# Late stores, four chunks ahead of the weights, and decay columns and more layouts by DMA in a fused decay-attention and feed-forward kernel

## The chip, the cores and the metric

One core of a Trainium2 chip. The metric is the device time of one execution in microseconds (us); a smaller one is better. The kernel before took 193.73 us (median of three runs, 192.81 to 193.88) in its first measurement. Its runs are of two kinds: those with a mean granted TensorE clock of 1.0 take 191.3 to 192.5 us, those with 0.99 mostly 192 to 194 us. So every comparison below is between runs of one session on one chip, and differences below half a percent are not read.

TensorE is PE below, VectorE DVE, ScalarE ACT, GpSimd POOL, SyncE SP. SP computes nothing here: it issues the loads of the operands, the transposes by DMA and (some of) the stores, one after the other in program order.

## The reference

Attention with a decayed state, 4 sequences, 8 heads, 768 steps, head size 48; then a feed-forward layer with squared ReLU.

```python
f = 1.0 / (1.0 + np.exp(-f_logit))
for t in range(S):
    state = f[:, :, t, :, None] * state + np.einsum('bhd,bhe->bhde', k[:, :, t], v[:, :, t])
    y[:, :, t] = np.einsum('bhd,bhde->bhe', q[:, :, t], state)
x = y.transpose(0, 2, 1, 3).reshape(B * S, H * D)      # 3072 x 384
h = np.maximum(x @ w_in, 0.0)                          # 384 -> 2048
return h * h @ w_out                                   # 2048 -> 384
```

## The kernel before

The 3072 steps are 24 chunks of 128, six to a sequence. `UNITS` says which chunks go through the first layer together, by first chunk and number. A small planner in the program takes each step of each chunk with its engine, its estimated length, its predecessors and the buffers that it takes and gives, and puts the instructions of all engines into one order. In the first 40 us it also puts "fillers" into PE's gaps: matmuls on zeros whose result nobody uses.

The order of loads. A weight slice (0.393 MB in the chip's type, four of `w_in`, four of `w_out`) is issued by POOL behind the cast of the v of the chunk named last but one before it:

```python
LOADS = [0, "i0", 1, "i1", 2, "i2", 3, "i3", 4, "o0", "o1", 5, "o2", "o3"] + list(range(6, NCH))
XBAR = 14      # from this chunk on, q and k are transposed by DMA and not by PE
XBAR2 = 18     # from this chunk on, the attention result is transposed by DMA
UNITS = [(0, 2), (2, 1), (3, 1), (4, 1), (5, 1)] + [(c, 3) for c in range(6, NCH, 3)]
# ... cut
plan.add(f"cw{kind}{s}", "POOL", 1.0, fn, after=[f"vc.{behind}"], rank=-1, data=(2.4, 0))
```

The decay. `pc` holds the running sum of log decays: 384 columns for the steps, and four one-column matmuls more that give the whole chunk's decay as a column for each pair of heads. One exponential on ACT turns all 388 columns into factors, DVE multiplies q with them, POOL multiplies the state by the last four.

```python
nc.tensor.matmul(pc[:, :HD], ut, pt[:, :, :D])
if not last:
    for pr in range(NP):
        nc.tensor.matmul(pc[:, HD + pr:HD + pr + 1], pt[:, 2 * pr:2 * pr + 2, :]..., ones)
# ... cut
nc.scalar.activation(st["en", i][:, :w], st["pc", i][:, :w], AFT.Exp, scale=-1.0)
# ... cut: the state update, on POOL
nc.gpsimd.tensor_mul(nx[r, ...], st["tm", i][r, ...], st["en", i][r, HD:HD + NP]...to_broadcast([D, NP, D]))
plan.add(f"s2.{i}", "POOL", 1.0, s2, after=[f"s1.{i}"] + ([f"p4.{i - 1}"] if c else []), ...)
```

The stores leave as each chunk is done, 18 through POOL and the last six through SP, from four output buffers:

```python
soft = i < NCH - 6
(nc.gpsimd if soft else nc.sync).dma_start(out[i * C:(i + 1) * C, :], st["ob", i])
```

## Time and profile before

| | before |
|---|---|
| median of the first session | 193.73 us (3 runs) |
| profiled run | 191.61 us, span 189.8 us, clock 1.000 |
| PE busy | 93% of the span, fillers included |
| PE work, from start-to-start times | 160.2 us |
| PE's last matmul ends, by the same count | 186.2 us |
| so PE lost | 26.0 us: 16.5 in 0 to 25 us, 6.7 in 25 to 50, 1.8 in 50 to 100, 1.0 after 100 |

The prediction below shows the lines that carry this. Two more are wanted for comparison, the rows of granted clock and of DMA bandwidth in 40 slices of the span of before (4.7 us each):

```profile
PEclk9999999999999999999999999999999999999999
GB/s 122 188 191 206 174 187 153 196 164 191 205 137 221 232 227 201 207 197 159 140 155 194 207 137 241 218 109 215 194 216 177 176 60 64 62 45 41 41 41 83
```

The clock is never throttled in this run, and the DMA engines move some 190 GB/s, 109 in the weakest slice, until slice 31.

### The profile page before, as it was taken

The page shows a single profiled execution, that of the slowest core. Times are in us where ns is not written, and L with a number is a line of the kernel's source. Part 1 is how long each engine was busy: PE and PEld are TensorE (multiplying, and loading weights), DVE is VectorE, ACT ScalarE, POOL GpSimd, SP SyncE. Part 2 cuts the span into 40 slices and gives each one's busy share as a digit, 9 for nine tenths or more (in the row PEclk, how much of TensorE's full clock was granted, in tenths as well). Part 3 has the DMA queues.
Part 4 walks back from the last instruction along what each step waited for, and adds up shares of the span by engine and source line. Part 5 has one row for each costly group of instructions (what it writes and reads, how often), then busy time and mean ns, then how long its engine had stood idle before and what let it go on. Part 6 is the DMA issues. An engine that isn't in the chain of part 4 may idle for free.

```text
span 189.8 us, 4807 instructions
## 1 busy us (share of the span) xinstructions
PE 177.5 (93%) x1845; PEld 120.8 (64%) x1845; DVE 127.6 (67%) x259; ACT 132.8 (70%) x281; POOL 54.8 (29%) x105
## 2 busy tenths in 40 slices
PE   6978689989899999999999999999999999999992
PEld 5867478767676666665656666666565666666551
DVE  5484688668397886999988777777667764343300
ACT  4426479786676469999998986978875787565521
POOL 5451343241224561305324311531324401100000
PEclk9999999999999999999999999999999999999999
DMA  6999899999979999999799999979999762211112
GB/s 122 188 191 206 174 187 153 196 164 191 205 137 221 232 227 201 207 197 159 140 155 194 207 137 241 218 109 215 194 216 177 176 60 64 62 45 41 41 41 83
DMA packets 118646, 30.26 MB, mean 159 GB/s; under 512 B 113408, under 2 KB 117760, under 8 KB 118624
## 3 DMA queue, kind: packets, MB, share of 16 engines
q1 hardware_dynamic: 113760, 23.27, 71.2%
q0 software_dynamic: 4864, 6.69, 16.4%
q8 instruction: 14, 0.23, 0.5%
q14 instruction: 8, 0.07, 0.1%
HBM read 25.17 MB, written 4.72 MB: 157 GB/s over the span
## 4 chain that ended last, share of the span: by engine, by line
PE 75%; ACT 11%; DMA 4%; SPq 3%; DVE 3%; issue 2%
PE op L489 31%; PE hp L444 30%; ACT hr L451 4%; DMA io_f<-in_f_logit_dram 4%; SPq L215 3%; PE at L342 3%; PE yp L365 3%; PE tr L318 2%; ACT hT L458 2%; PE pc L286 2%; PE xp L379 1%; PE ds L405 1%; ACT pz L276 1%; ACT e L275 1%; DVE hr L453 1%
## 5 line engine op out<-in xcount | busy, mean ns | idle before, releaser
L444 PE MATMUL hp<-xT,w_in 128*128 128x384 bf16 (+2 forms) x528 | 78.0, 282 | 2.5 <-DVE hr L453 1.9
L489 PE MATMUL op<-w_out,hT 128*128 128x384 bf16 x384 | 76.2, 326 | 0.3 <-ACT ob L499 0.3
L451 ACT ACTIVATE hr<-hp 128x384 bf16<-128x384 f32 (+1 forms) x100 | 50.5, 509 | 20.0 <-PE hp L444 18.0
L444 PEld LDWEIGHTS <-w_in 128*128 128x128 bf16 x528 | 42.3, 98 | 20.7 <-issue 4.0
L489 PEld LDWEIGHTS <-hT 128*128 128x128 bf16 x384 | 35.1, 98 | 21.8 <-issue 0.4
L460 DVE TENSOR_TENSOR hT<-hr 128x384 bf16<-128x384 bf16 (+1 forms) x75 | 29.7, 400 | 27.7 <-ACT hr L451 26.8
L349 DVE TENSOR_TENSOR am<-at,ut 128x512 bf16<-128x512 f32 x48 | 31.6, 685 | 3.7 <-PE at L342 3.4
L422 POOL TENSOR_TENSOR sz<-tm,en 48x192 bf16<-48x192 f32 x40 | 22.0, 549 | 29.9 <-DVE tm L413 7.2
L458 ACT ACTIVATE hT<-hr 128x384 bf16<-128x384 bf16 (+1 forms) x45 | 24.8, 554 | 1.6 <-DVE hr L453 0.3
L504 POOL DMA_DIRECT2D out_dram<-ob x18 | 10.4, 577 | 47.3 <-ACT ob L499 31.2
L280 POOL CAST vz<-io_v 128x384 bf16<-128x384 f32 x24 | 13.6, 567 | 31.2 <-DMA io_v<-in_v_dram 30.7
L306 DVE TENSOR_TENSOR az<-io_k,ep 128x384 bf16<-128x384 f32 x24 | 14.0, 584 | 8.3 <-ACT ep L296 5.1
L275 ACT ACTIVATE e<-io_f 128x384 f32<-128x384 f32 x24 | 12.5, 520 | 7.7 <-DMA io_f<-in_f_logit_dram 7.7
L499 ACT COPY ob<-op 128x384 f32<-128x384 f32 x18 | 8.6, 478 | 12.8 <-PE op L489 12.7
L296 ACT ACTIVATE ep<-pc 128x384 f32<-128x384 f32 x24 | 11.7, 486 | 5.8 <-PE pc L289 5.4
L310 DVE TENSOR_TENSOR az<-io_q,en 128x384 bf16<-128x384 f32 x24 | 14.7, 614 | 0.0
L276 ACT ACTIVATE pz<-e 128x384 bf16<-128x384 f32 x24 | 12.5, 523 | 0.8
L453 DVE TENSOR_SCALAR hr<-hp 128x384 bf16<-128x384 f32 (+1 forms) x20 | 11.6, 584 | 2.0 <-PE hp L444 1.8
L522 PE MATMUL idle<-zero 128*128 128x128 bf16 x119 | 11.9, 256 | 1.0 <-DVE zero L245 1.0
L302 ACT ACTIVATE en<-pc 128x388 f32<-128x388 f32 (+1 forms) x24 | 11.8, 491 | 0.0
L326 DVE COPY ts<-tr 128x1024 bf16<-128x1024 bf16 x14 | 9.6, 687 | 3.1 <-PE tr L318 2.7
L365 PE MATMUL yp<-vz,am 128*128 128x48 bf16 x192 | 9.5, 184 | 1.3 <-DVE am L349 0.8
(40 smaller groups left out, 149.4 us busy)
## 6 DMA issues: line engine op xcount, KB each, us to landing
io_f<-in_f_logit_dram SPq DMA_DIRECT2D x24, 192.0 KB, 4.5
io_k<-in_k_dram SPq DMA_DIRECT2D x24, 192.0 KB, 4.6
io_q<-in_q_dram SPq DMA_DIRECT2D x24, 192.0 KB, 4.5
io_v<-in_v_dram SPq DMA_DIRECT2D x24, 192.0 KB, 4.5
out_dram<-ob POOLq DMA_DIRECT2D x18, 192.0 KB, 3.5
w_in<-in_moe_w_in_dram POOLq DMA_DIRECT2D x4, 384.0 KB, 7.4
w_out<-in_moe_w_out_dram POOLq DMA_DIRECT2D x4, 384.0 KB, 6.9
out_dram<-ob SPq DMA_DIRECT2D x6, 192.0 KB, 1.9
```

The costliest lines, as they stand in the source:

```text
L275: nc.scalar.activation(e, st["f", i].rearrange("p h d -> p (h d)"), AFT.Exp, scale=-1.0)
L276: nc.scalar.activation(pz[i % 2][:, :, :D], e.rearrange("p (h d) -> p h d", d=D), AFT.Ln, bias=1.0)
L306: nc.vector.tensor_mul(az[i % 4][:, H:, :D], st["k", i], st["ep", i])
L310: nc.vector.tensor_mul(az[i % 4][:, :H, :D], st["q", i], st["en", i][:, :HD].rearrange("p (h d) -> p h d", d=D))
L349: nc.vector.tensor_mul(t, st["at", i][x], ut4)
L365: nc.tensor.matmul(o_, w, r, start=(n == 0), stop=(n == len(ops) - 1), skip_group_check=True)
L422: nc.gpsimd.tensor_mul(nx[r, :, D * x:D * (x + 1)], st["tm", i][r, :, D * x:D * (x + 1)], st["en", i][r, HD:HD + NP].unsqueeze(2).to_broad ...
L444: nc.tensor.matmul(hp[:, x, :], w_in[:, ks, (f + x) * C:(f + x + 1) * C], xT[:, ks, lo:lo + W], start=(ks == 0), stop=(ks == KS - 1), skip ...
L451: nc.scalar.activation(hr[:, :m, :], st["hp", c0, f][:, :m, :], AFT.Relu)
L458: nc.scalar.activation(st["hT", g][:, f:f + m, lo:lo + W], hr[:, :m, :], AFT.Square)
L460: nc.vector.tensor_mul(st["hT", g][:, f:f + m, lo:lo + W], hr[:, :m, :], hr[:, :m, :])
L489: nc.tensor.matmul(st["o", i], hT[:, fs, tt * C:(tt + 1) * C], w_out[:, fs, :], start=(fs == 0), stop=(fs == FS - 1))
```

## The change

Its intent: take 2.6 us of small matmuls and transposes from PE and let the DMA engines do them, pay for their time by moving the stores behind the last load, and give PE more attention work at the start by loading four chunks before any weight.

```diff
-    LOADS = [0, "i0", 1, "i1", 2, "i2", 3, "i3", 4, "o0", "o1", 5, "o2", "o3"] + list(range(6, NCH))
+    LOADS = [0, 1, 2, 3, "i0", "i1", "i2", "i3", "o0", "o1", 4, "o2", "o3"] + list(range(5, NCH))
-    XBAR = 14
-    XBAR2 = 18
-    UNITS = ... + [(c, 3) for c in range(6, NCH, 3)]
+    XBAR = 12
+    GX = 9
+    XBAR2 = 14
+    UNITS = ... + [(c, 3) for c in range(6, NCH - 3, 3)] + [(c, 1) for c in range(NCH - 3, NCH)]
 ... the column matmuls of the decay
-            if not last:
+            if not last and i < GX:
 ... the exponential, from chunk 9: written transposed, so that its last row can be sent to a column
+                t = t.rearrange("p (x d n) -> p x d n", x=2, n=NP)
+                t, st["row", i] = t[:, :, :D].rearrange("p x d n -> p n x d"), t[C - 1:C]
+                nc.scalar.activation(t, st["pc", i][:, :HD]..., AFT.Exp, scale=-1.0)
 ... the transfer
+        def tg():
+            t = st["g", i] = work.tile([C, NP], F32, tag="g", bufs=3, name="g")
+            nc.sync.dma_start(t, st["row", i].rearrange("o x d n -> o (x d) n"))
+        if i >= GX:
+            plan.add(f"tg.{i}", "SP", 0.45, tg, after=[f"a2n.{i}"], take=["g"], rank=-2, data=(0.2, 128))
 ... the stores: all on SP, behind the last load, from 20 buffers (OBB) instead of 4
-                (nc.gpsimd if soft else nc.sync).dma_start(out[i * C:(i + 1) * C, :], st["ob", i])
+                nc.sync.dma_start(out[i * C:(i + 1) * C, :], st["ob", i])
-            plan.add(f"d{i}", "POOL" if soft else "SP", ..., after=[f"e{i}"], rank=-1, ...)
+            plan.add(f"d{i}", "SP", 0.45, dma, after=[f"e{i}", f"v{LATE}"], rank=1, ...)
```

Cut: buffers for the exponential and for g, three planning lengths on PE, and a test in the planner's model of the DMA queue.

More of the change, by code (lines that the diff above doesn't have):

```diff
@@ L113, in order @@
                         us, size = s.data
-                        while sum(z for e, z in queue if e > end) + size > self.RING:
+                        while size and sum(z for e, z in queue if e > end) + size > self.RING:
                             end = min(e for e, z in queue if e > end)
@@ L175 @@
     NCH = B * NC
+    LATE = NCH - 1
+    OBB = 20
     IOB = 7
     HTB = 3
-    LOADS = [0, "i0", 1, "i1", 2, "i2", 3, "i3", 4, "o0", "o1", 5, "o2", "o3"] + list(range(6, NCH))
+    LOADS = [0, 1, 2, 3, "i0", "i1", "i2", "i3", "o0", "o1", 4, "o2", "o3"] + list(range(5, NCH))
     LOADS = [x if isinstance(x, int) else (x[0], int(x[1])) for x in LOADS]
     FILL = 40.0
-    XBAR = 14
-    XBAR2 = 18
-    UNITS = [(0, 2), (2, 1), (3, 1), (4, 1), (5, 1)] + [(c, 3) for c in range(6, NCH, 3)]
+    XBAR = 12
+    GX = 9
+    XBAR2 = 14
+    UNITS = [(0, 2), (2, 1), (3, 1), (4, 1), (5, 1)] + [(c, 3) for c in range(6, NCH - 3, 3)] + [(c, 1) for c in range(NCH - 3, NCH)]
     GC = 3
@@ L198 @@
     plan.buffers(**{"io_" + n: IOB for n in "fkqv"})
-    plan.buffers(m=2, tr=1, at0=1, at1=1, h=2, o=1, hr=3, hT=HTB, xT=2, ob=4,
-                pz=2, az=4, vz=4, ts=3, am=2, ys=3, ep=2, en=4)
+    plan.buffers(m=2, tr=1, at0=1, at1=1, h=2, o=1, hr=3, hT=HTB, xT=2, ob=OBB,
+                pz=2, az=4, vz=4, ts=3, am=2, ys=3, ep=2, en=4, g=3)
     st = {}
@@ L254 @@
         nc.gpsimd.tensor_copy(ut4[:, j, :], ut)
-    pz, az, vz, sz = [], [], [], []
+    pz, az, vz, sz, ez = [], [], [], [], []
     for j in range(2):
@@ L263 @@
         nc.vector.memset(az[j], 0.0)
+        ez.append(const.tile([C, H * DP], F32, name=f"ez{j}"))
+        nc.gpsimd.memset(ez[j], 0.0)
         vz.append(const.tile([C, H, D], BF16, name=f"vz{j}"))
@@ L291, in p1 @@
             st["pc", i] = pc
-        plan.add(f"p1.{i}", "PE", 0.26, p1, after=[f"a1.{i}"] + ([f"p4.{i - 3}"] if i > 2 else []), take=["m"], give=[f"pz:a1.{i}"], rank=rank)
+        plan.add(f"p1.{i}", "PE", 0.26 if i < GX and not last else 0.165, p1, after=[f"a1.{i}"] + ([f"p4.{i - 3}"] if i > 2 else []), take=["m"], give=[f"pz:a1.{i}"], rank=rank)
         def a2p():
@@ L299, in a2n @@
         def a2n():
-            w = HD if last else HD + NP
-            st["en", i] = work.tile([C, HD + NP], F32, tag="en", bufs=4, name="en")
-            nc.scalar.activation(st["en", i][:, :w], st["pc", i][:, :w], AFT.Exp, scale=-1.0)
+            t = ez[i % 4]
+            if i < GX:
+                w = HD if last else HD + NP
+                nc.scalar.activation(t[:, :w], st["pc", i][:, :w], AFT.Exp, scale=-1.0)
+                st["en", i], st["g", i] = t[:, :HD].rearrange("p (h d) -> p h d", d=D), t[:, HD:HD + NP]
+            else:
+                t = t.rearrange("p (x d n) -> p x d n", x=2, n=NP)
+                t, st["row", i] = t[:, :, :D].rearrange("p x d n -> p n x d"), t[C - 1:C]
+                nc.scalar.activation(t, st["pc", i][:, :HD].rearrange("p (n x d) -> p n x d", x=2, d=D), AFT.Exp, scale=-1.0)
+                st["en", i] = t
         plan.add(f"a2n.{i}", "ACT", 0.37, a2n, after=[f"p1.{i}", f"a2p.{i}"], take=["en"], give=[f"m:p1.{i}"])
@@ L309, in v1q @@
         def v1q():
-            nc.vector.tensor_mul(az[i % 4][:, :H, :D], st["q", i], st["en", i][:, :HD].rearrange("p (h d) -> p h d", d=D))
+            t, z = st["q", i], az[i % 4][:, :H, :D]
+            if i >= GX:
+                t, z = (y.rearrange("p (n x) d -> p n x d", x=2) for y in (t, z))
+            nc.vector.tensor_mul(z, t, st["en", i])
         plan.add(f"v1q.{i}", "DVE", 0.47, v1q, after=[f"a2n.{i}", f"q{i}", f"v1k.{i}"], give=[f"io_q:q{i}"] + ([f"en:a2n.{i}"] if last else []))
@@ L344, in p3 @@
             st["am", i] = [None, None]
-        plan.add(f"p3.{i}", "PE", 0.34, p3, after=[f"v2.{i}"], take=["at0", "at1"], rank=rank)
+        plan.add(f"p3.{i}", "PE", 0.42, p3, after=[f"v2.{i}"], take=["at0", "at1"], rank=rank)
         def v3(x):
@@ L366, in p4 @@
             st["yp", i] = yp
-        plan.add(f"p4.{i}", "PE", 0.38 if c else 0.2, p4, after=[f"v3b.{i}", f"vc.{i}"] + ([f"s2.{i - 1}"] if c else [])
+        plan.add(f"p4.{i}", "PE", 0.37 if c else 0.2, p4, after=[f"v3b.{i}", f"vc.{i}"] + ([f"s2.{i - 1}"] if c else [])
                  + ([] if last else [f"p5.{i}"]),
@@ L422, in s2 @@
                 nc.gpsimd.tensor_mul(nx[r, :, D * x:D * (x + 1)], st["tm", i][r, :, D * x:D * (x + 1)],
-                                     st["en", i][r, HD:HD + NP].unsqueeze(2).to_broadcast([D, NP, D]))
-        plan.add(f"s2.{i}", "POOL", 1.0, s2, after=[f"s1.{i}"] + ([f"p4.{i - 1}"] if c else []), give=[f"en:a2n.{i}"])
+                                     st["g", i][r].unsqueeze(2).to_broadcast([D, NP, D]))
+        def tg():
+            t = st["g", i] = work.tile([C, NP], F32, tag="g", bufs=3, name="g")
+            nc.sync.dma_start(t, st["row", i].rearrange("o x d n -> o (x d) n"))
+        if i >= GX:
+            plan.add(f"tg.{i}", "SP", 0.45, tg, after=[f"a2n.{i}"], take=["g"], rank=-2, data=(0.2, 128))
+        plan.add(f"s2.{i}", "POOL", 1.0, s2, after=[f"s1.{i}"] + ([f"p4.{i - 1}"] if c else []) + ([f"tg.{i}"] if i >= GX else []),
+                 give=[f"en:a2n.{i}"] + ([f"g:tg.{i}"] if i >= GX else []))
     def mm1(c0, n):
@@ L497, in ev, with dma @@
             def ev(e, i=i):
-                ob = st["ob", i] = ffp.tile([C, d_model], F32, tag="ob", bufs=4, name="ob")
+                ob = st["ob", i] = ffp.tile([C, d_model], F32, tag="ob", bufs=OBB, name="ob")
                 copy[e](ob, st["o", i])
-            soft = i < NCH - 6
-            def dma(i=i, soft=soft):
-                (nc.gpsimd if soft else nc.sync).dma_start(out[i * C:(i + 1) * C, :], st["ob", i])
+            def dma(i=i):
+                nc.sync.dma_start(out[i * C:(i + 1) * C, :], st["ob", i])
             both(f"e{i}", 0.46, 0.37, ev, after=[f"o{i}.4"], take=["ob"], give=[f"{tag}:o{i}.0"])
-            plan.add(f"d{i}", "POOL" if soft else "SP", 1.0 if soft else 0.45, dma, after=[f"e{i}"], give=[f"ob:e{i}"], rank=-1, data=(0.6, 0 if soft else 128))
+            plan.add(f"d{i}", "SP", 0.45, dma, after=[f"e{i}", f"v{LATE}"], give=[f"ob:e{i}"], rank=1, data=(0.6, 128))
     for i in range(NCH):
```

## The prediction

> **What bounds the kernel now.** I read the page's shares first, then the waits of the TensorE, then its timeline, then the DMA queues in the first 50 us. The page:
>
> ```profile
> PE 177.5 (93%) x1845; PEld 120.8 (64%) x1845; DVE 127.6 (67%) x259; ACT 132.8 (70%) x281; POOL 54.8 (29%) x105
> ...
> DMA  6999899999979999999799999979999762211112
> ```
>
> TensorE (PE) is busy 93%, but 11.9 us of that are fillers (the group idle<-zero, x119), all before 40 us. The DMA row is full until slice 31 (about 150 us) and nearly empty after it. So there are two regimes: a start in which PE has too little to do because operands and weights are still coming, and a long stretch in which PE is the bound. The waits of PE alone confirm it; these are the largest two of all:
>
> ```profile
> PE hp L444 <- DVE hr L453: 1.9, 1, 1.9
> PE pc L286 <- ACT pz L276: 1.8, 3, 1.0
> ```
>
> Both lie before 30 us. Between 50 and 187 us PE stands idle in the records for under 1 us (busy 49.64 of 50, 50.00 of 50, 36.40 of 37). A busy PE need not be at its peak, so I check by start-to-start times in the PE timeline (columns: start, length, line, operation, count):
>
> ```profile
> 50.61 0.83 PE L444 MATMUL hp<-xT,w_in 128*128 128x128 bf16 x12
> 51.28 1.14 PE L489 MATMUL op<-w_out,hT 128*128 128x384 bf16 x6
> ...
> 53.41 0.61 PE L318 MATMUL tr<-ident,az 128*128 128x128 bf16 x8
> 53.86 0.33 PE L405 MATMUL ds<-vz,az 128*128 128x96 bf16 x4
> ...
> 59.60 0.24 PE L289 MATMUL pc<-ones,pz 128*128 128x1 bf16 x4
> 59.71 0.33 PE L379 MATMUL xp<-ident,ys 128*128 128x128 bf16 x3
> ...
> 178.44 7.96 PE L489 MATMUL op<-w_out,hT 128*128 128x384 bf16 x48
> ```
>
> Twelve 128-column matmuls take 51.28 - 50.61 = 0.67 us, 56 ns each; the last 48 of 384 columns take about 163 ns each. Both scale with columns, so nothing but issue stands between them: PE streams. From 49.67 us to its last matmul at 186.4 us it has 136.8 us, of which I count 133 us as matmuls at such rates; the rest is mostly 0.1 us ahead of each chunk's L342. **What counts is therefore PE work after the start plus what PE fails to do in the start.** Loads, stores, DVE and ACT count only if they starve PE.
>
> **What the skill says.** (1) "Perfetto Trace Analysis", Identifying the Most-Contended Engine: matmul busy share is a poor measure, weight-load share a better one. Here that is 64% against 93%; 384-column matmuls need one load each, so I trust the start-to-start times. (2) "TensorE: Matmul & The Clock Gate", section "Wait — 56ns, not 53.3ns?": 128 columns cost 55.6 ns warm, columns at 2.4 GHz plus about 2.5 ns. The trace agrees: 56 ns. (3) "DMA: Bandwidth & Descriptors", Queues, rings and completion order: each DMA engine takes turns between queues at packet granularity, so a queue with large packets gets more bytes. The trace agrees in direction, in the queue view of 10 to 18 us, where the first three weight slices (software queue) run beside operand loads (hardware queue); columns are packets, MB, time share:
>
> ```profile
> q0 software_dynamic: 1117, 1.11, 83.3%
> q1 hardware_dynamic: 2330, 0.44, 36.6%
> ```
>
> Weights move 0.139 MB/us, loads 0.055 MB/us, against 0.18 to 0.19 for loads alone. (4) Same page, "Issuing engines are not separate DMA queues": moving a DMA to another issuer saves only issue time. No run shows this yet; I use it for the stores.
>
> **The change, part by part.**
>
> Decay by DMA from chunk 9. The four one-column matmuls (L289) cost 59.71 - 59.60 = 0.11 us a chunk. They go in chunks 9 to 22 except 11 and 17 (a sequence's last chunk has none): 12 x 0.105 = **-1.26 us** of PE. A tiny DMA per chunk takes their place, and the state update waits for it. Median landing of other DMAs on that queue is 4 to 5 us in this busy phase, but chunks come some 6 us apart and other matmuls fill the wait.
>
> Operand transposes by DMA from chunk 12 instead of 14: eight matmuls cost 53.86 - 53.41 = 0.45 us; two chunks, **-0.90 us**. Two DVE copies of 0.69 us go too, off the path. Result transposes from chunk 14 instead of 18: 0.17 us each (three 56 ns matmuls), four chunks, **-0.68 us**.
>
> Last three chunks one at a time: 144 matmuls of 128 columns replace 48 of 384. Per 384 columns 3 x 56 = 168 ns instead of 163, plus rounding: some **+0.24 us**. The last group may start before chunk 23 is through, but PE already had work there (no wait after 150 us), so this gains nothing.
>
> Sum: -1.26 - 0.90 - 0.68 + 0.24 = **-2.6 us of PE in the saturated stretch**.
>
> Stores after the loads. 18 stores leave POOL, where each issue took 0.58 us. They took 3.54 MB out of the loaded phase; at about 0.19 MB/us plus the lighter cost of their large packets I estimate 10 us of DMA, against some 7 us for two more operand and four more result transposes (1.7 and 0.9 us, the kernel's own plan; an estimate). Loads end a few us earlier. PE was not waiting for loads, so: **0**. In the tail 24 stores of 0.2 MB in 35 us are no load; the last store is unchanged.
>
> Four chunks ahead of the weights. POOL's timeline of before, casts of v and weight issues:
>
> ```profile
> 7.02 0.50 POOL L280 CAST vz<-io_v 128x384 bf16<-128x384 f32 x1 [3.50 <-DMA io_v<-in_v_dram]
> 7.46 1.69 POOL L231 DMA_DIRECT2D w_in<-in_moe_w_in_dram  x2
> ...
> 21.63 0.94 POOL L280 CAST vz<-io_v 128x384 bf16<-128x384 f32 x1 [6.62 <-DMA io_v<-in_v_dram]
> 22.51 0.80 POOL L231 DMA_DIRECT2D w_in<-in_moe_w_in_dram  x1
> 27.33 0.51 POOL L280 CAST vz<-io_v 128x384 bf16<-128x384 f32 x1 [0.24 <-DMA io_v<-in_v_dram]
> 27.78 1.55 POOL L233 DMA_DIRECT2D w_out<-in_moe_w_out_dram  x2
> ```
>
> Weight slices were let go by the casts of chunks 0, 0, 1, 2, 3, 3, 4, 4; now all six first ones wait for chunk 2 and the last two for chunk 3. Chunks 0 and 1 landed 4.2 us apart undisturbed, so chunk 2 now lands near 15.5 us, not 21.6. Weights then flow from about 18 us (packets came 2 us after issue), w_in complete after 4 x 0.393 / 0.139 = 11.3 us: 29.5 us (before: about 29). w_out moved 0.80 MB in 8 us per pair, so it ends near 45.5 us (before: 46). The total is the same; the order is the difference. What PE can do meanwhile: attention of 0 to 3 is through by 22 us, about 4 us earlier. But the first ReLU on ACT comes behind chunk 4's exponential in program order, and f of chunk 4, squeezed to 0.055 MB/us, lands only near 27 us. I expect PE to stall around 23 to 28 us, then to run full until it waits for the last w_out slices near 41 to 45 us. PE work done at 46 us: attention 0 to 4 (9 us), first layer of 0 to 4 (13 us), second layer of chunk 0 (2.6 us), 24.5 us; before it was about 25. **0 within 3 us.** I choose 0.3 us of gain, from fewer small waits; the choice is weak.
>
> Total: 193.7 - 2.6 - 0.3 = **190.8 us**.
>
> **Rivals.** (a) The start gains 3 to 4 us: if loads keep a larger share beside the weights, chunk 4 lands by 24 us, the ReLUs are not blocked, and PE enters saturation with more done. For it: weights in the w_out phase left loads 0.07 to 0.08 MB/us, and fewer back-and-forth waits. Then 187 to 188. (b) The start loses: six weights in a row starve chunks 3 and 4, and the blocked ACT and DVE hold the two hp buffers, as DVE did at 19.5 us (the 1.9 us wait). Then 193 to 195. (c) A new wait replaces the removed work: the decay DMA, queued in order behind loads on SP, delays the state update and so L365, or SP stands waiting for it and loads come late; chunk 23's transposes stand behind up to 16 stores. For it: f of chunk 23 was issued at 142.6 and used at 148.3 us, no great lead. Against: PE found other work through all such waits before. Up to +2 us. (d) The removed matmuls hid under others: against it stand the start-to-start times above.
>
> **Range and chances.** The PE sum is safe to 0.5 us; the start carries +-3 us, new waits up to +2. Hence 187.5 to 194.0. Faster by over 2% needs 189.86 or less, 0.9 us below my centre: 0.36. Slower by over 2% needs 197.6, three things failing at once: 0.04. Within 2%: 0.60.
>
> **What would show it.** Right: L289's count 80 to 32, tr 112 to 96, xp 54 to 42; PE still without waits from 50 us to the end; PE's last matmul about 2.5 us earlier; DMA row emptying earlier, then stores. Fillers and waits before 46 us about equal in sum, with a gap at 23 to 28 us. Wrong: PE saturated before 42 us or only after 50 us; PE waits on L365, L342 or on sz after 90 us; a gap near the end behind a chunk 22 or 23 transpose.

## More of the kernel before

"PE work" is a count: each matmul at the start-to-start time that its shape shows in the busy stretch (0.163 us for 384 columns, 0.109 for 256, 0.056 for 128, 0.0265 for one column, and so on), fillers at nothing. What is left of the time until PE's last matmul is "lost". Work plus loss is the end, so a change that takes work away gains only if the loss stays.

## The result

The changed kernel took 195.38 us (median of 4 runs, 195.06 to 195.61), the kernel before 193.41 us (4 runs, 192.81 to 193.88) on the same chip. The ratio is 1.010, with a 95% interval of 1.007 to 1.014: 1% slower, where 1.5% faster was predicted, and outside the predicted range. A later session gave 1.011 (1.005 to 1.018).

| | before | after |
|---|---|---|
| profiled span, clock | 189.8 us, 1.000 | 193.3 us, 0.982 |
| PE work | 160.2 us | 157.6 us |
| PE lost, 0 to 25 us | 16.5 | 18.4 |
| 25 to 50 us | 6.7 | 7.6 |
| 50 to 100 us | 1.8 | 4.4 |
| after 100 us | 1.0 | 1.5 |
| last load issued | 147.8 us | 154.5 us |

The work fell by 2.6 us, exactly as predicted. The loss rose by 5.8 us in the profiled runs. The profiled run of before was a quick one (191.61 us, against a median of 193.41); by the medians, 2.0 us slower with 2.6 us less work, the loss rose by some 4.6 us. From the page of the changed kernel, shares and the rows that answer to those of before:

```profile
PE 178.8 (93%) x1861; PEld 124.0 (64%) x1861; DVE 128.8 (67%) x252; ACT 132.3 (68%) x274; POOL 47.5 (25%) x91
...
PEclk9999969879999999999999999999999999999999
DMA  6999999999999944979997799979988989671012
GB/s 119 192 178 173 175 189 185 184 169 202 169 196 167 178 73 84 194 145 169 158 203 145 124 197 167 153 152 175 151 158 168 154 216 293 223 271 43 33 52 79
```

The shares say nothing: PE is 93% busy in both. The rows say where to look: a clock that falls in slices 5 to 8 (24 to 43 us), and a hole in the DMA row at slices 14 and 15 (68 to 77 us), while loads are still wanted. PE's largest waits in the changed kernel (who waited, for what, us in total, times, longest):

```profile
PE tr L333 <- DVE az L325: 2.6, 1, 2.6
PE hp L467 <- DMA w_in<-in_moe_w_in_dram: 1.9, 1, 1.9
```

The first layer waits for its first weights, at 24.3 us, where it started at 17.1 us in before (its matmuls on `w_in` up to 60 us, before and after: ns at least, in the median, at most; first and last start):

```profile
L444 PE MATMUL hp<-xT,w_in x240: 216/219/283, 17.1 to 56.0; 128*128 128x128 bf16 x96, 128*128 128x256 bf16 x24
L467 PE MATMUL hp<-xT,w_in x192: 216/219/421, 24.3 to 50.5; 128*128 128x128 bf16 x144, 128*128 128x256 bf16 x48
```

Then the transposes of chunk 4 wait for their operand, at 37.4 us. POOL's timeline of the changed kernel shows the cause of both (start, length, operation; idle time before):

```profile
16.34 0.51 POOL L285 CAST vz<-io_v 128x384 bf16<-128x384 f32 x1 [1.68 <-DMA io_v<-in_v_dram]
16.88 3.24 POOL L234 DMA_DIRECT2D w_in<-in_moe_w_in_dram  x4
20.12 1.52 POOL L236 DMA_DIRECT2D w_out<-in_moe_w_out_dram  x2
...
23.26 1.54 POOL L236 DMA_DIRECT2D w_out<-in_moe_w_out_dram  x2
...
42.20 0.51 POOL L285 CAST vz<-io_v 128x384 bf16<-128x384 f32 x1 [12.91 <-DMA io_v<-in_v_dram]
```

The chunk 2 cast comes at 16.3 us, near the predicted 15.5. Then all eight slices are asked for within 8 us, and the v of chunk 4 lands only at 42.2 us, against 36.9 us in before. The DMA queues of the changed kernel, 24 to 30 us (packets, MB, share of the time):

```profile
q0 software_dynamic: 974, 0.95, 93.2%
q1 hardware_dynamic: 969, 0.18, 27.8%
```

The two queues moved the same number of packets, 974 and 969 (and 1174 each in 30 to 36 us). That agrees with the turn by packets that the Trainium skill describes in "DMA: Bandwidth & Descriptors", Queues, rings and completion order, though a profile's packet need not be what the page calls one, and how many go in one turn is not seen. With weights always outstanding, loads get one packet of 190 bytes for every weight packet of 980 (both are means), 0.03 MB/us. The prediction took 0.055 MB/us from a window in which loads had moved two packets for each weight packet, because the weight queue was empty at times.

The wait itself is not all. In the windows of the changed kernel around the two waits (start:end, length, busy time and count by engine, then granted clock, DMA share, GB/s):

```profile
22.00:28.00 6.00, 4.07 (x49) 3.48 (x48) 2.85 (x6) 1.90 (x4) 2.66 (x5) 0.72 1.21 191
28.00:36.00 8.00, 6.38 (x85) 5.53 (x83) 3.02 (x8) 7.01 (x14) 1.04 (x2) 1.00 1.26 186
36.00:42.00 6.00, 4.58 (x42) 3.68 (x43) 3.46 (x7) 1.80 (x4) 0.00 (x0) 0.72 1.25 194
```

A mean of 0.72 over 6 us fits half a clock for 3.4 us (1 - 0.5 x 3.4 / 6 = 0.72). In before the clock is 1.00 in these three windows. Both dips follow a wait of 2 to 3 us.

The hole at 68 to 77 us. SP's largest wait but one, and SP's timeline across it, in the changed kernel:

```profile
SPq L443 <- ACT ez L313: 8.3, 5, 5.9
```

```profile
66.16 1.01 SPq L218 DMA_DIRECT2D io_k<-in_k_dram  x1
73.11 0.56 SPq L443 DMA_DIRECT2D g<-ez  x1
73.76 0.54 SPq L218 DMA_DIRECT2D io_q<-in_q_dram  x1
```

SP stands 5.9 us at the first decay transfer, for the exponential of chunk 9, and the loads behind it in the program wait as well. And the exponential in the transposed layout is dear. The exponential of before and after, then DVE's multiplication of q, after and before (busy us, mean ns; then idle time before):

```profile
L302 ACT ACTIVATE en<-pc 128x388 f32<-128x388 f32 x20 | 9.9, 493 | 0.0
```

```profile
L313 ACT ACTIVATE ez<-pc 128x384 f32<-128x384 f32 x15 | 13.1, 876 | 0.0
L325 DVE TENSOR_TENSOR az<-io_q,ez 128x384 bf16<-128x384 f32 x24 | 18.8, 785 | 4.3 <-DMA io_q<-in_q_dram 3.3 <-ACT ez L313 0.8
```

```profile
L310 DVE TENSOR_TENSOR az<-io_q,en 128x384 bf16<-128x384 f32 x24 | 14.7, 614 | 0.0
```

ACT takes 876 ns in place of 493, and DVE's multiplication of q 845 to 870 ns in most of chunks 9 to 23 in place of 551, the median of before (785 and 614 are means, and mix quick and slow ones). 15 chunks by 0.38 and by 0.3 us are 5.7 us of ACT and 4.5 us of DVE. Neither is the bound over the whole span, but in 70 to 90 us DVE is busy 19.5 of 20 us (17.7 in before).

### The profile page after: what moved, and what is told of

Same layout as the page of the kernel before. It is cut to its first block, busy times and chain, and to the rows that moved or that the text cites. A ratio compares the mean times of both kernels' runs of the same rounds, so it can differ in the third digit from the quotient of the medians.

```text
span 193.3 us, 4827 instructions
## 1 busy us (share of the span) xinstructions
PE 178.8 (93%) x1861; PEld 124.0 (64%) x1861; DVE 128.8 (67%) x252; ACT 132.3 (68%) x274; POOL 47.5 (25%) x91
## 4 chain that ended last, share of the span: by engine, by line
PE 65%; DMA 9%; SPq 9%; DVE 8%; ACT 5%; issue 2%; DVEq 0%
PE op L512 30%; PE hp L467 24%; DMA io_q<-in_q_dram 9%; SPq L218 9%; PE yp L380 3%; PE at L357 3%; DVE am L364 2%; ACT hr L474 2%; DVE az L325 2%; PE tr L333 2%; PE pc L291 1%; PE ds L420 1%; ACT ob L522 1%; DVE az L318 1%; ACT hT L481 1%
## 5 line engine op out<-in xcount | busy, mean ns | idle before, releaser
L467 PE MATMUL hp<-xT,w_in 128*128 128x128 bf16 (+2 forms) x624 | 78.5, 271 | 2.5 <-DMA w_in<-in_moe_w_in_dram 1.9
L467 PEld LDWEIGHTS <-w_in 128*128 128x128 bf16 x624 | 48.5, 100 | 21.1 <-issue 2.4
L483 DVE TENSOR_TENSOR hT<-hr 128x384 bf16<-128x384 bf16 (+1 forms) x78 | 32.0, 415 | 27.3 <-ACT hr L474 26.1
L437 POOL TENSOR_TENSOR sz<-tm,g 48x192 bf16<-48x192 f32 x24 | 13.8, 574 | 33.9 <-DVE tm L428 16.6
L325 DVE TENSOR_TENSOR az<-io_q,ez 128x384 bf16<-128x384 f32 x24 | 18.8, 785 | 4.3 <-DMA io_q<-in_q_dram 3.3
L481 ACT ACTIVATE hT<-hr 128x384 bf16<-128x384 bf16 (+1 forms) x38 | 20.5, 545 | 1.4 <-DVE hr L476 0.6
L437 POOL TENSOR_TENSOR sz<-tm,ez 48x192 bf16<-48x192 f32 x16 | 8.3, 516 | 24.7 <-DVE tm L428 14.0
L313 ACT ACTIVATE ez<-pc 128x384 f32<-128x384 f32 x15 | 13.1, 876 | 0.0
L333 PE MATMUL tr<-ident,az 128*128 128x128 bf16 x96 | 8.9, 231 | 3.0 <-DVE az L325 2.6
L388 ACT CAST ys<-yp 128x384 bf16<-128x384 f32 x17 | 8.2, 483 | 4.0 <-PE yp L380 4.0
```

Of the source, the lines that this page charges most:

```text
L313: nc.scalar.activation(t, st["pc", i][:, :HD].rearrange("p (n x d) -> p n x d", x=2, d=D), AFT.Exp, scale=-1.0)
L325: nc.vector.tensor_mul(z, t, st["en", i])
L437: nc.gpsimd.tensor_mul(nx[r, :, D * x:D * (x + 1)], st["tm", i][r, :, D * x:D * (x + 1)], st["g", i][r].unsqueeze(2).to_broadcast([D, NP, D]))
L467: nc.tensor.matmul(hp[:, x, :], w_in[:, ks, (f + x) * C:(f + x + 1) * C], xT[:, ks, lo:lo + W], start=(ks == 0), stop=(ks == KS - 1), skip ...
L481: nc.scalar.activation(st["hT", g][:, f:f + m, lo:lo + W], hr[:, :m, :], AFT.Square)
L483: nc.vector.tensor_mul(st["hT", g][:, f:f + m, lo:lo + W], hr[:, :m, :], hr[:, :m, :])
```

## The experiments

18 kernels, in five sessions, each session on one chip and with its own runs of the kernel before. First two names. **START**: four chunks ahead of the weights cost time before 45 us. **DECAY**: the decay by DMA costs more, on ACT, DVE and SP, than the PE work that it saves. Rivals are that the clock alone, the stores or the layouts by DMA are the cause. The planner is one as well: each edit also moves other instructions.

### First session: parts undone

`a_loads_before`: the changed kernel with the old order of loads.

```diff
-    LOADS = [0, 1, 2, 3, "i0", "i1", "i2", "i3", "o0", "o1", 4, "o2", "o3"] + list(range(5, NCH))
+    LOADS = [0, "i0", 1, "i1", 2, "i2", 3, "i3", 4, "o0", "o1", 5, "o2", "o3"] + list(range(6, NCH))
```

> The changed kernel with the old order of weights and chunks alone. Theory S (the start loses: eight weight slices in flight leave the loads 0.03 MB/us, PE waits 2.1 us for w_in and 2.7 us for q of chunk 4, and its clock halves after each): PE lost 24.7 us before 50 us after the change and 22.9 before it (end minus work), so 2 to 5 us come back: 190.5 to 193.5, clock 1.0, no wait of PE over 2 us. Rival M (only the middle, 50 to 95 us, counts): 195, within 0.5.

Measured: 191.22 us, ratio 0.996 (0.989 to 1.003). The result was wrong (relative error 0.050).

`a_decay_pe`: `GX = NCH`, so that TensorE makes the decay in all chunks.

> The changed kernel with the decay back on PE in all chunks (no transposed write of the exponential, no small DMA). Theory M (the transposed layout makes ACT's exponential 0.88 instead of 0.49 us and DVE's product 0.89 instead of 0.6, and DVE and ACT are full from 70 to 100 us): the 2.5 us lost between 50 and 95 us come back, 1.26 us of PE work are added: 193.5 to 194.5. Rival S alone: 196.3 to 196.8.

Measured: 197.34 us, ratio 1.026 (1.018 to 1.035). Wrong result (0.043).

`a_loads_before_decay_pe`: both edits.

> Both undone; transposes from 12 and 14, late stores and single last chunks stay. If S and M are both right and add: 190.5 to 192, faster than before by 1 to 1.5%. If the rest of the change also costs something: 193 or more.

Measured: 190.21 us, ratio 0.990 (0.981 to 0.998). Wrong result (0.043).

The wrong results were not meant. They repeat, digit for digit, in a simulation, and sit in one chunk: 17 in the first, 11 in the others, the last of a sequence. The cause is a hole in the planner's constraints that the kernel before has too. The first chunk of a sequence writes the state buffer that the last chunk of the sequence before still reads, and the constraint between them is left out `if c` is zero. In before and after the order happens to come out right; in these three it did not. It also made a wait that is no part of the question, in the trace of `a_decay_pe`:

```profile
PE yp L380 <- POOL sz L437: 2.3, 1, 2.3
```

So the 197.34 us is not used. One edit mends it, and is in all kernels from the second session on:

```diff
-        after=[f"s1.{i}"] + ([f"p4.{i - 1}"] if c else [])
+        after=[f"s1.{i}"] + ([f"p4.{i - 1}"] if i else [])
```

`a_fill_waits`: the changed kernel with idle matmuls (36 and 46) in the program ahead of the two long waits, so that PE does not stand.

```diff
+            if i == 4:
+                st["fill"](46)
 ...
+                if c0 == 0 and f == 0:
+                    st["fill"](36)
```

> The changed kernel with 36 fillers ahead of the first first-layer matmul and 46 ahead of chunk 4's transposes, where PE waits anyway. If the halved clock after the two waits costs time of its own: clock 1.0 and 2 to 3 us less, 192.5 to 193.5. If only the waits themselves cost: 195 to 195.5 although the clock is 1.0.

Measured: 193.56 us, ratio 1.007 (1.000 to 1.015), correct, clock 1.0 in the profile; PE's last matmul ended at 188.5 us in place of 189.5 us. The profiled runs thus put the halved clock at about 1 us. The ratios, 1.007 here and 1.010 for the changed kernel, have intervals that overlap, so this size is not shown. The clock is not the whole of the loss: PE's loss by 50 us stays at 25.3 us, against 26.0 in the changed kernel.

### Second session: the same, safe

`c_after_again`: the changed kernel with the safe order. The instructions of every engine are the same as without it, so it is the control.

> The changed kernel with one more line of order in its planner (the state of the first chunk of a sequence is written after the last chunk of the sequence before has read that buffer). The instructions come out identical to those of the changed kernel on every engine, so this is the control of this batch: 195 us, ratio to the kernel before 1.01, granted clock below 1 in most runs, about 32 us of PE time lost. If it is 1.00 or below here, the +1% of the first measurement was the chip and the day and not the kernel.

`c_loads_before`: with the old order of loads.

> The changed kernel with the old order of loads (weights between the chunks), and with the order of the state buffer made safe, so a correct result this time. Theory START (four chunks ahead of the weights, and so eight slices at once, cost the first 45 us): 191.0 us against 195 for the control, a ratio to before of 0.995, clock 1.0, lost PE time down by 3 to 4 us, all of it before 45 us. Rival DECAY (the cost is all in the middle, from the layout of the exponential): 194 to 195, as the control.

`c_decay_pe`: with the decay by TensorE.

> The changed kernel with the decay columns made by TensorE in all chunks as before (no transposed layout of the exponential, no decay transfers), loads as changed, order of the state buffer made safe. The first try of this at 197.3 us had a false wait of 2.3 us and a wrong result from that order. Theory DECAY: PE work rises by 60 matmuls of 0.021 us, 1.3 us, while ACT and DVE lose 0.4 and 0.3 us per chunk over 14 chunks, and SP no longer stands at chunk 9; if that standing and strided layout cost PE 2.5 us, the sum is 193.5 to 194.5. Rival START alone: 195 + 1.3 = 196 or more, the middle loses as little as it would anyway.

`c_both`: with both.

> Old order of loads and decay by TensorE, with the order made safe: what is left of the change is late stores, 20 output buffers, and operands and results laid out by DMA from chunks 12 and 14. START and DECAY both true: 190 us, ratio to before 0.985 to 0.99, lost PE time as before (26 us) and PE work 1.3 us below before. If only START is true: 192 (the loads' 191 plus 1.3 of PE work). This is the candidate to beat both kernels.

Measured, all correct; before 191.99 us (11 runs):

| kernel | median us | ratio | 95% interval | PE lost by 50 us | 50 to 100 us | last load issued |
|---|---|---|---|---|---|---|
| c_after_again | 194.07 | 1.011 | 1.005 to 1.018 | 24.7 | 4.3 | 152.3 |
| c_loads_before | 192.16 | 1.000 | 0.995 to 1.005 | 24.6 | 3.8 | 151.1 |
| c_decay_pe | 194.41 | 1.011 | 1.006 to 1.016 | 25.7 | 3.6 | 150.3 |
| c_both | 190.62 | 0.992 | 0.987 to 0.997 | 22.2 | 2.2 | 144.3 |

The profile of `c_loads_before` is of its slowest run, 193.1 us (its fastest took 190.9), so its losses are some 2 us above those of its better runs, and only the times of that kernel are read.

START holds: the old order of loads gives back 1.1% with the decay by DMA, 1.9% without it. Where the time goes is seen in `c_decay_pe` and `c_both`, which differ in LOADS alone: 3.5 us of more loss by 50 us, and 1.4 us from 50 to 100 us. DECAY holds with the old loads, with intervals that just overlap: giving the 1.3 us of matmuls back to PE makes the kernel 0.8% faster (1.5 us of median), so the decay by DMA cost some 2.8 us where the prediction had only its gain. (The matmuls are 48, in 12 chunks, and not the 60 of the expectation.) With the new loads, though, DECAY comes out even, at 1.011 both times. The costs do not add. I read the reason in SP's waits of `c_decay_pe`, where another instruction, the first transpose of operands by DMA, stands for the same time, some 12 us later (issued at 84.9 us, the decay transfer of the changed kernel at 73.1):

```profile
SPq L344 <- DVE az L325: 11.2, 7, 5.9
```

With the new loads the attention of the middle chunks is late whatever makes the decay (DVE is busy 19.6 of 20 us in 70 to 90 us here, 18.7 in `c_both`), and SP, in order, stands at the first instruction that needs it. That this is why they do not add is argued, and no run shows it alone.

### Third session: parts alone, and what in DECAY costs

`d_loads_alone`: the kernel before with the new LOADS only.

> The kernel before with one part of the change alone: four chunks ahead of the weights (and the state buffer's order made safe, which leaves the kernel before itself identical). START: the four gains of the change are absent, the loss of the start is there: 194 us, ratio to before 1.01 to 1.015, a granted clock below 1 after the waits at 20 to 40 us, and DVE busy over 95% in 70 to 90 us because the attention work of the first chunks is late and piles up there. Rival (the order of loads costs only together with the rest of the change): ratio 1.000 to 1.004.

Measured: 195.68 us, ratio 1.018 (1.014 to 1.022) from five runs. The sixth, the one with the profile, took 447.86 us: PE busy 99%, 432 ns from start to start for 384 columns in place of 163, 187 for 128 in place of 56, at a recorded clock of 1.0. I have no cause for that one run, and its trace is not used, so the expected sign in DVE (over 95% busy in 70 to 90 us) was not seen or refuted. START is now shown from both sides in the times. That the part alone costs more than the whole change (1.018 against 1.010) is as it should be where the rest takes PE work away.

`d_xbar_alone`: the kernel before with `XBAR = 12`, `XBAR2 = 14`.

> The kernel before with operands laid out by DMA from chunk 12 and results from chunk 14, alone. By the working on record PE loses 16 transposes of operands and 12 of results, 1.6 us less 0.2 us for the odd chunks: 190.5 us, ratio 0.992 to 0.994, PE work 1.3 to 1.6 us below, loss unchanged at 26 us. Rival (the extra DMA time of the transfers delays loads): 192, ratio 1.00. It should equal the version with old loads and decay by TensorE (0.992) if late stores and 20 output buffers are worth nothing.

Measured: 194.37 us, ratio 1.009 (1.003 to 1.014): a loss, where a gain of 0.7% was expected. PE work fell by 1.6 us as counted; the loss of PE rose from 26.0 to 30.7 us, and 3.1 us of the rise lie after 100 us. See the fourth session.

`d_flat_decay`: the changed kernel with old loads; the exponential stays in its plain layout and four transfers carry its last row.

```diff
-            nc.sync.dma_start(t, st["row", i].rearrange("o x d n -> o (x d) n"))
+            for n in range(NP):
+                nc.sync.dma_start(t[:, n:n + 1], st["row", i][:, n * C:(n + 1) * C])
```

> The changed kernel with the old order of loads, and with the exponential left in its plain layout: the decay columns are then carried by four small transfers per chunk in place of one, ACT and DVE keep their contiguous 0.49 and 0.61 us. Theory LAYOUT (the transposed layout, 0.39 us more on ACT and some 0.3 on DVE per chunk, is what ate the 1.3 us): 189.3 us, the 190.6 of decay by TensorE less 1.3 of PE work. Theory QUEUE (the transfer stands in the SP queue behind the exponential and holds up loads): 192, as with the old loads and one transfer, or worse with four issues of 0.5 to 1 us.

Measured: 202.78 us, ratio 1.052 (1.046 to 1.057). The exponential is back at 493 ns and the multiplication at 550 ns (median), so the layout alone makes those times. But four issues take 2.5 to 3.1 us of SP per chunk, and what stands behind them is late; SP's timeline, and PE's largest wait, in this run:

```profile
85.74 2.55 SPq L442 DMA_DIRECT2D g<-ez  x4
88.40 1.25 SPq L342 DMA_TRANSPOSE ts<-az  x1
```

```profile
PE at L355 <- DMA ts<-az: 6.4, 7, 2.1
```

It does not say how much the layout costs, since it brought a larger cost of the other kind. It shows how dear time on SP is.

`d_pool_decay`: the changed kernel with old loads; the one transfer is issued by POOL.

```diff
-            nc.sync.dma_start(t, st["row", i].rearrange("o x d n -> o (x d) n"))
+            nc.gpsimd.dma_start(t, st["row", i].rearrange("o x d n -> o (x d) n"))
```

> The changed kernel with the old order of loads and the decay transfer issued by POOL in place of SP, the transposed layout kept. Theory QUEUE: SP stands no more at the exponential: 189.5 us. Theory LAYOUT: 192, as with the transfer on SP. If both are 190.5 to 191, each of the two costs some 1 us.

Measured: 191.59 us, ratio 0.996 (0.991 to 1.000), between `c_loads_before` (1.000) and `c_both` (0.992), with intervals that overlap both. How the 2.8 us of DECAY divide between the layout and SP's standing stays open.

### Fourth session: why layouts by DMA lost alone, and doses

`e_xbar_units`: `d_xbar_alone` with the last three chunks as units of one.

> The kernel before with operands and results laid out by DMA from chunks 12 and 14 (as the run that did this alone, 194.4 us) and the last three chunks as units of one each. Theory UNITS (its 3 us of lost PE time after 100 us come from the last unit of three, whose first layer waits for each chunk in turn): 191 us, ratio 0.993, PE lost after 100 us back at 1 us. Theory STORES (SP and the transfers are held up by the early stores): 194, no change.

Measured: 193.02 us, ratio 1.005 (0.999 to 1.010). PE lost 2.4 us after 100 us, against 4.1.

`e_both_old_units`: `c_both` with the old UNITS.

> The best version so far (old loads, decay by TensorE, late stores with 20 buffers, operands and results by DMA from 12 and 14; 190.6 us, ratio 0.992) with the old units, three chunks to the end. Theory UNITS: 193.5 us, ratio 1.007, the loss in the last 90 us at 4 us in place of 0.8. Theory STORES: 190.6, no change, since what helped was that the stores no longer lie between the loads.

Measured: 190.20 us, ratio 0.988 (0.982 to 0.993). Not the 193.5 us of theory UNITS. The units of one are no part of the gain when stores are late; when stores are early they may help a little. STORES is left, and what speaks for it is the last load on SP, in the timelines of before, of `d_xbar_alone` and of `e_both_old_units`:

```profile
147.77 0.53 SPq L215 DMA_DIRECT2D io_v<-in_v_dram  x1
```

```profile
157.53 0.53 SPq L215 DMA_DIRECT2D io_v<-in_v_dram  x1
```

```profile
145.60 0.53 SPq L218 DMA_DIRECT2D io_v<-in_v_dram  x1
```

This pair does not differ in stores alone: `e_both_old_units` is made from the changed kernel and keeps its planning lengths, its test in the planner and its buffers for the exponential. Run without a chip on `d_xbar_alone`, the planner puts the last load at 154.8 us; with the new lengths and test at 153.5, with late stores in their place at 143.9. These are its own times and no measurement, but by them it is the stores that move the last load. That they alone make the difference in time, 1.009 against 0.988, no run shows.

With early stores, the additional transposes push the last load back by 10 us. The attention of chunk 23 then ends at 169.6 us instead of 160.2 us, and after it PE has one unit of feed-forward left and nothing to mix with it: in `d_xbar_alone` it waits, from start to start, 0.6 us at 172.8 us for the last transposed result and 0.25 us before each of four groups of matmuls after that. With late stores the last load comes 2 us earlier than in before, in spite of the same transposes.

`e_paced`: `c_both` with four chunks ahead, and the `w_out` slices spaced.

```diff
+    LOADS = [0, 1, 2, 3, "i0", "i1", "i2", "i3", 4, "o0", 5, "o1", 6, "o2", 7, "o3"] + list(range(8, NCH))
```

> The best version so far with the changed kernel's four chunks ahead of the weights, but the w_out slices spaced: one after each of chunks 4 to 7, in place of all eight slices within 7 us. Theory IN FLIGHT (eight slices at once leave the loads too small a share of the DMA engines between 24 and 36 us): 191 us, ratio 0.993 to 0.997, against 194.4 with the eight together (ratio 1.011). Theory LATE (whatever is done, w_in behind four chunks keeps the first layer waiting): 194, ratio 1.01.

Measured: 196.02 us, ratio 1.019 (1.013 to 1.025). The v of chunk 4 is cast at 35.5 us and no more at 41.5 as in `c_decay_pe`, and PE's longest wait is shorter (1.6 us in place of 3.2). But the first layer still waits for `w_in` until 24.0 us, and later chunks and `w_out` come in each other's way: PE loses 5.8 us in 50 to 100 us. So fewer slices in flight shorten the waits but win little back: PE lost 25.2 us by 50 us, against 25.7 in `c_decay_pe` and 22.2 in `c_both`. LATE fits: in either version the first layer starts at 23 to 24 us where it starts at 17 us with the old loads, and until then PE has attention work alone. It is not shown alone, since `e_paced` also brings `w_out` later, and no run delays `w_in` alone.

`e_gx16`: `c_both` with `GX = 16`.

> The best version so far with the decay by DMA in chunks 16 to 23 alone: 7 chunks by 4 matmuls of 0.021 us, 0.6 us less PE work. If ACT and DVE have the slack there (both under 80% busy after 110 us in the trace of the best version) and SP stands only where no load is awaited: 190.0 us, ratio 0.989. If SP's standing at the exponential holds up loads there too: 191 to 192.

Measured: 189.87 us, ratio 0.987 (0.983 to 0.992), correct. No loss where ACT and DVE have slack (six chunks and 24 matmuls, and not the seven chunks of the expectation); against `c_both`'s 0.992 the intervals overlap, so a gain is not shown.

### Fifth session: stores alone, and the parts that helped together

`f_stores_alone`: the kernel before with late stores and 20 buffers. It is made from the changed kernel with the other parts set back, so it too keeps the planning lengths, the test in the planner and the buffers for the exponential.

> The kernel before with the late stores alone (all 24 stores on SP after the last load, 20 output buffers); loads, decay, units and layout by DMA as before. By the prediction on record: 0, 192.4 us, since PE waited for no load. If the stores are what the two layouts by DMA need (without late stores these lost 0.9%, with them and the old units they gained 1.2%) but nothing by themselves, also 0: ratio 0.997 to 1.003. If late stores are themselves worth the difference of 2%, ratio 0.98.

Measured: 191.46 us, ratio 0.994 (0.987 to 1.000). The last load is issued at 135.4 us in place of 147.8. PE has no use for most of these 12 us, as predicted. The layouts by DMA fit into them: alone they cost 0.9%, here they cost nothing. That they gain anything beside late stores is not shown, since the versions with both (0.987 to 0.992) have intervals that overlap this one's.

`f_best`: old loads, old units, late stores, `XBAR = 12`, `XBAR2 = 14`, `GX = 16`.

> Old loads, old units, late stores with 20 buffers, operands and results by DMA from chunks 12 and 14, decay by DMA from chunk 16 alone. The two halves were 0.9878 (old units) and 0.9872 (decay from 16); units of one cost 0.25 us of PE work by the count: 189.6 us, ratio 0.985, if they add; 0.988 if they do not.

Measured: 191.11 us, ratio 0.989 (0.983 to 0.996), correct. The parts do not add up further. `c_both`, `e_both_old_units`, `e_gx16` and `f_best` are one group at 0.987 to 0.992 within their intervals: all beat the kernel before by about 1%, and the changed kernel by about 2%. Each has the old order of loads, late stores, and layouts of operands and results by DMA from chunks 12 and 14.

## Why the prediction was wrong

- **PE work, -2.6 us: right.** 160.2 to 157.6 us. Counts of the small matmuls and transposes came out as written (80 to 32, 112 to 96, 54 to 42).
- **The start, "0 within 3 us": the step that failed.** Its cost alone is 1.8% of 192 us, 3.4 us, and 1.1% to 1.9% within the rest of the change. The prediction put PE's work done at 46 us at 24.5 us, against about 25 before. By the count of this document it was 20.0 us, against 24.3. The reasoning had the order of events right (chunk 2 at 16.3 us, a stall at 24 us) and three things wrong. The loads' share beside the weights was taken as 0.055 MB/us from a window in which the weight queue had gaps; it was 0.03, one packet for one packet; f of chunk 4 came in time all the same (used at 24.2 us), but its q only for 37.4 us. The sum of PE work took the stalls as filled by other work; PE waited 1.9 and 2.6 us, and its first layer started 7 us later than in before. And the clock after such waits, about 1 us of PE in the profiled runs, was not foreseen. How the loss divides between the late first layer and the starved loads stays open. Rival (b), 193 to 195 us, named the starved loads and nearly the right time; PE's waits for hp buffers, its other half, were 0.4 us.
- **Decay by DMA, "-1.26 us": the gain right, the cost left out.** The text priced the transfer's landing. It did not price the layout that the transfer asks for (0.38 us on ACT, 0.3 on DVE for each of 15 chunks) nor, except as a rival of up to 2 us, the place of the transfer in SP's order. The Trainium skill, "SBUF — State Buffer", Door 1, says that accesses that stay in one 16-byte line run at full bandwidth and each new line costs. In the transposed layout each fp32 element lies 16 bytes from the next, so the times agree (876 ns in place of 493 on ACT; 493 again in `d_flat_decay`), and it was there to be read. With the old loads the two together ate 2.8 us. "PE found other work through all such waits before" was said against this, and did not hold.
- **Layouts by DMA, "-0.90" and "-0.68 us": right as work, wrong as a term that stands by itself.** Alone they cost 0.9%. With late stores they cost nothing; whether they give a part of the gain of 1% is within the noise.
- **Stores, "0": about right alone** (0.6%, interval to 0). The 10 us do not follow from what is written (3.54 / 0.19 is 18.6, and the discount for large packets isn't worked out), but the last load came 12 us sooner, and 10 us later with the layouts alone, so the balance of 10 against 7 had the right sign. It was written down as a zero, though the room that it makes is what the layouts need.
- **"Loads, stores, DVE and ACT count only if they starve PE"**: true, and the prediction then assumed that they do not. Before issues f of its last chunk at 142.6 us and uses it at 148.3, which the prediction itself had noted as "no great lead". In the profiled runs the versions whose last load is issued at 152 us or later (among them after, `d_xbar_alone`, `e_xbar_units`) all lose or are even; those at 149 us or earlier are all at 0.987 to 0.994, but for `e_paced`, which loses at the start, and before itself (147.8 us); between 150 and 152 us it goes either way (1.011, 1.000, 0.996, the last by a slow run's trace). That the two go together does not show which makes which.

The whole: -2.6 us of work, and 5.8 us of new loss in the profiled runs, of which 2.8 before 50 us (START), 2.6 in 50 to 100 us (late attention from START, and DECAY) and 0.5 after. In the medians the new loss is some 4.6 us. How the second of these divides is not settled, because START and DECAY do not add.

## What to carry to other kernels

In a kernel where PE is the bound, count the PE work that a change takes away, and then ask separately for each queue that issues in order what it will stand at, and how much lead the last load keeps: here the layouts moved to DMA cost 0.9% with early stores and nothing with late ones, so make room first, then move layouts. Two queues that take turns by packet share bytes by packet size, and the share must be read in a window in which both are always full. A new layout must be priced at its producers and consumers, not only at the transfer that it serves.

## What the Trainium skill lacked or had wrong

- "TensorE: Matmul & The Clock Gate", What's actually happening, has a halved clock after an idle window of about 3.4 us. Here waits of 2.1 and 2.7 us (by start-to-start times) were each followed by half the clock for about 3.4 us, and with fillers over them the clock stayed at 1.0. A wait of 1.9 us in before was not.
- "SBUF — State Buffer", Door 1, gives 4 fp32 elements as how far one can stride for free, which can be read as allowing a stride of four. At such a stride, 16 bytes, each element is in a new line, and it was not free: ACT's exponential took 876 ns in place of 493 with it, DVE's multiplication about 855 in place of 551. The page has no figure for either engine.
- "DMA: Bandwidth & Descriptors", Issuing engines are not separate DMA queues, calls the issue time that another engine saves usually small. The time that SP stands in order before an issue is not named there: 5.9 us at one transfer, with the DMA engines down to 73 and 84 GB/s; and four tiny issues a chunk in place of one, 2.5 to 3.1 us of SP, came with 5% of the kernel's time.
- No page that I found has the figures of, or a cause for, a run like the one of 447.86 us: 432 ns for 384 columns and 187 for 128, in place of 163 and 56, at a recorded clock of 1.0.
